# Whole V tile to the third buffer, all of wo to the first, in the tail of a decode-attention kernel

## The chip, the cores and the metric

The kernel runs on one core of one Trainium2 chip. The metric is device time in microseconds (us); the time shown for a version is the median of several executions. A profile is one further execution, recorded by the hardware profiler, and has a time of its own.

Engines are named as in the profile: PE is the matmul engine and PEld its weight load, DVE the vector engine, ACT the scalar engine, POOL the general one, SP the engine that issues nearly all transfers between HBM and on-chip memory. Each engine works through its own list of instructions in order; between engines, and between engines and transfers, order is kept by counters (semaphores) on which an instruction waits.

## The reference, cut to what matters

One decode step of a transformer block with attention and a feed-forward branch side by side: batch B = 4, one query each, D = 512, H = 32 heads of Dh = 128, a cache of Sk = 8192 keys and values per head, F = 1792, all bf16.

```python
xn = _layernorm(x)
q = (xn @ wq).reshape(B, 1, H, Dh).transpose(0, 2, 1, 3)
scores = einsum("bhqd,bhkd->bhqk", q, k_cache) * Dh ** -0.5
p = softmax(scores)
o = einsum("bhqk,bhkd->bhqd", p, v_cache)
attn = o.transpose(0, 2, 1, 3).reshape(B, 1, H * Dh) @ wo
ffn = (silu(xn @ w_gate) * (xn @ w_up)) @ w_down
out = x + attn + ffn
```

The K and V caches hold 537 MB together, and each of their elements is read once. Nearly all of the 550.77 MB that the kernel reads is theirs.

## The kernel before, in words

**Tiles.** The 128 pairs of batch and head are worked on in 32 head groups of four heads (`NT` = 32, `LAST` = 31). One group's K is one tile of 128 partitions by 32768 bf16 (64 KB a partition, 8.39 MB), and so is its V. Three buffers of that size, `slot[0]` to `slot[2]` (line 77), hold whatever is being loaded or used; K of group n and V of group n go to slot n mod 3, one after the other. Everything else is small.

**One step.** For group n, `begin` (line 353) turns K in place with DVE, piece by piece (`turn_k`, line 268), and PE computes the scores from each piece (`score`, line 275). Then `load_v` (line 97) issues the load of V into the slot that K has left. `finish` of the same group (line 364) takes the row maximum (`max_1`), multiplies the group before's probabilities with its V (`pv`, line 317: 64 matmuls, number k reading columns 512k to 512k+511 of the slot, the first 16 ahead of `max_2`, the other 48 behind it), issues the load of K of group n+2 into the slot that this V has left (`load_k`, line 94), and then turns its own probabilities (`pt_turn`) and finishes the group before's output (`fin`). So a step holds `finish(n)`, `begin(n+1)` and `load_v(n+1)`.

**Order and loop.** The order of the instructions is written out by hand (`manual_schedule`, line 70). The steps lie in a loop of 11 trips, n = 0, 3, ..., 30 (line 383). It has two arms: for n below 30, three steps (line 386); for n = 30, the tail (line 390), which holds the rest. All of SP's transfers go through one queue in program order, and each load of a slot waits until the slot's last readers are done.

**The waits.** The framework sets the waits. It follows which part of a buffer each instruction reads or writes, and makes a later access wait for an earlier one. A transfer's landing is seen by a completion counter; SP's transfers take eight counters in turn. At the loop's end both arms join, so that what the next trip meets is what either arm may have left. A wait that reaches across the loop's end is expressed as the value that the counter has when the trip before is over.

**The tail before.** `finish(30)` multiplies with V29 from slot 2. Then the first half of V31 (`va`, line 410) is loaded to the upper half of slot 2; once K31's first scores are done, its second half (`vb`, line 413) goes to the lower half of slot 1, and wo (`load_wo`, `load_wo_heads`, lines 396 and 400) in eight pieces to the lower half of slot 2, heads 0 to 31 at 512 columns each. Behind these loads in program order come the rest of group 30 (`max_1`, `pv` with V30 from slot 0, `max_2`, `fin`), `pv` with V31, and the output projection `wo_mm` (line 403), eight of whose heads stand between the two halves of the last `fin`. Two copies and two transfers write the result.

Of the kernel before, what the change touches and what calls it, by code (L numbers as in the profile page):

```python
# [15 lines left out]
def kernel(  # L16
# [13 lines left out]
    nc = tc.nc  # L30
    P = nc.NUM_PARTITIONS

    B, Sq, D = A_x.shape
    _, H, Sk, Dh = A_k_cache.shape
# [8 lines left out]
    T = HT * Sk // P  # L43
# [28 lines left out]
    def mm(out_ap, lhsT, rhs, start, **kw):  # L72
        nc.tensor.matmul(out_ap, lhsT=lhsT, rhs=rhs, start=start, stop=True,  # L73
                         skip_group_check=True, **kw)

    pad_t = pad.tile([P, 64], dt.bfloat16, name="pad_t")
    slot = [slots.tile([P, SLOT], dt.bfloat16, name=f"slot{i}") for i in range(NSLOT)]
    k_all = A_k_cache.rearrange("b (j h) (p t) d -> (b j) (h p) (t d)", h=HT, t=T)
    v_all = A_v_cache.rearrange("b (j h) (p t) d -> (b j) (h p) (t d)", h=HT, t=T)
# [17 lines left out]
    def load_v(n, s):  # L97
        nc.sync.dma_start(out=slot[s][:], in_=v_all[bass.ds(n, 1), :, :].rearrange("o p f -> (o p) f"))
# [5 lines left out]
                      in_=x_flat[B - 1:B, :].rearrange("b (k e) -> b k e", k=2))  # L104
# [43 lines left out]
    def yo_mm(lhsT, rhs, start=False):  # L148
        for i in range(2):
            mm(yo_ps[i][i * QB:i * QB + B, :], lhsT, rhs[:, i * DH:(i + 1) * DH], start=start)  # L150
# [39 lines left out]
    for half in range(NH):  # L190
        for par in range(2):
            src = q_ps[half][:].rearrange("p (x i r) -> p x i r", x=8, r=2)[:, :, :, par]
            src = src.unsqueeze(2).to_broadcast([P, 8, NQ, QB])
# [13 lines left out]
    for half in range(NH):  # L207
        for par in range(2):
            for a in range(HT):
                q0, q1 = a * QB, (a + 1) * QB  # L210
                nc.vector.tensor_copy(
                    out=qtn[q0:q1, :].rearrange("p (b h c j r) -> p h r j c b", b=B, h=NH, c=NQ, j=2)[:, half, par],
                    in_=qt_ps[q0:q1, half, par, 2 * a:2 * a + 2, :].rearrange("p j (c b) -> p j c b", b=B))
# [42 lines left out]
    NK = T // NV  # L256
    LAST = NT - 1
# [19 lines left out]
    def max_1():  # L277
        mx = small.tile([P, 1], dt.float32, name="mx")
        nc.vector.reduce_max(out=mx[:], in_=sps[:], axis=AX.X)  # L279
        return mx  # L280

    def max_2(mx):

        nc.tensor.matmul(mps[:, 0:P], lhsT=mx[:, 0:1].to_broadcast([P, P]), rhs=ident_f[:, :],  # L284
                         is_transpose=True, start=True, stop=True, skip_group_check=True)
        nm = small.tile([P, HT], dt.float32, name="nm")
        nc.vector.tensor_reduce(out=nm[:], in_=by_row(mps[:, 0:P]), axis=AX.X, op=ALU.max, negate=True)  # L287
        nc.vector.tensor_tensor(out=nm[:], in0=nm[:], in1=rowb_q[:], op=ALU.mult)
        nb = small.tile([P, 1], dt.float32, name="nb")
        nc.vector.reduce_sum(out=nb[:], in_=nm[:], axis=AX.X)  # L290
        rs = small.tile([P, 1], dt.float32, name="rs")
        nc.scalar.activation(out=p_[:], in_=sps[:], func=ACT.Exp, bias=nb[:, 0:1], scale=qscale,  # L292
                             accum_out=rs[:])
        return rs

    def pt_turn():
        for y in range(HT):
            nc.vector.transpose(out=ptz[y * QB:(y + 1) * QB, :, y, :, :].rearrange("p s u x -> p s (u x)"),  # L298
                                in_=p_[y * QB:(y + 1) * QB, :].rearrange("p (s w) -> p s w", s=4))
# [3 lines left out]
    def row_sums(rs):  # L303
        mm(mps[:, P:P + HT], rs[:, 0:1].to_broadcast([P, P]), rowb[:], start=True)

    def recip(c):
        nc.vector.reciprocal(out=rcp[c % NSLOT][:], in_=mps[:, P:P + HT])  # L307

    def p_off(k):
        g, s_ = divmod(k, TG // NV)  # L310
        return s_ * HT * NV * QB + 2 * g

    def pv(v, k0, k1):

        for k in range(k0, k1):
            q0, off = (k % NQ) * QB, p_off(k)
            mm(o_acc[q0:q0 + WR, :], pt[:, off:off + (WR - 1) * QB + 1:QB], v(k), start=(k < NQ))

    def in_slot(s):
        return lambda k: slot[s][:, k * 512:(k + 1) * 512]  # L320
# [17 lines left out]
    def fin(n, c, between=None):  # L338
        fin_1()
        if between:  # L340
            between()
        scaled(n, c, fin_2())

    def turned(j0, j1):

        xq = psX.tile([P, 4, B, j1 - j0], dt.float32, name="xps")
        src = otn_nat[:, HT:].rearrange("p (b j y) -> p b j y", b=B, y=HT)
        for y in range(HT):
            for c in range(4):
                mm(xq[y * QB:(y + 1) * QB, c, :, :], ident[:, c:P:4], src[:, :, j0:j1, y], start=(c == 0))  # L350
        nc.vector.tensor_copy(out=otn[:, j0 * 4:j1 * 4, :].rearrange("p (j c) b -> p c b j", c=4), in_=xq[:])

    def begin(n, c, parts=(4, 4, 2, 2, 2, 2), head=False):
        build_q(n)
        if head:
            mm(sps[0:1, 0:1], zq[:, 0, 0:1], zq[:, 0, 0:1], start=True)
        g0 = 0
        for w in parts:
            turn_k(c % NSLOT, g0, (w,))
            for g in range(g0, g0 + w):  # L360
                score(c % NSLOT, g)
            g0 += w

    def finish(n, c, load=True):
        sp = (c - 1) % NSLOT
        mx = max_1()
        pv(in_slot(sp), 0, 16)
        rs = max_2(mx)
        pv(in_slot(sp), 16, NK)
        if load:  # L370
            load_k(n + 2, sp)
        row_sums(rs)
        pt_turn()
        recip(c)
        fin(n - 1, c - 1)
# [7 lines left out]
    with tc.For_i(0, NT + 1, NSLOT, iteration_sync="reg_based", hint_engines=[]) as n:  # L383
        with tc.If(n < NT - 2) as turn:
            n = nc.s_assert_within(n, 0, NT - 2 - NSLOT, skip_runtime_bounds_check_because="the arm has n < NT - 2")
            for c in range(NSLOT):
                finish(n + c, c)
                begin(n + c + 1, c + 1)
                load_v(n + c + 1, (c + 1) % NSLOT)
        with turn.Else():  # L390
            finish(LAST - 1, LAST - 1, load=False)

            wo_t = slot[2]

            def load_wo(k0, k1):
                nc.sync.dma_start(out=wo_t[:, k0 * 4 * D:k1 * 4 * D].rearrange("p (k c e) -> p k (c e)", c=4, e=D),
                                  in_=A_wo[k0 * 4 * P:k1 * 4 * P, :].rearrange("(k p c) e -> p k (c e)", p=P, c=4))

            def load_wo_heads(h0, h1):
                nc.sync.dma_start(out=wo_t[:, h0 * D:h1 * D].rearrange("p (h e) -> p h e", e=D),  # L400
                                  in_=A_wo[h0 * P:h1 * P, :].rearrange("(h p) e -> p h e", p=P))

            def wo_mm(i):
                lhsT = otn[:, i, :] if i < H - HT else otn_nat[:, HT:].rearrange("p (b h) -> p b h", b=B)[:, :, i]
                yo_mm(lhsT, wo_t[:, i * D:(i + 1) * D])

            TH = T // 2
            va, vb = slot[2][:, H * D:H * D + TH * Dh], slot[1][:, 0:TH * Dh]
            src = v_all[LAST]
            nc.sync.dma_start(out=va, in_=src[:, 0:TH * Dh])  # L410
            turned(0, NB4 - 2)
            begin(LAST, LAST, (2,) * 8)
            nc.sync.dma_start(out=vb, in_=src[:, TH * Dh:T * Dh])
            for k0, k1 in ((0, 2), (2, 4), (4, 5), (5, 6), (6, 7)):
                load_wo(k0, k1)
            for h0, h1 in ((H - 4, H - 2), (H - 2, H - 1), (H - 1, H)):
                load_wo_heads(h0, h1)
            v30 = in_slot(0)
            mx = max_1()
            pv(v30, 0, 16)  # L420
            rs = max_2(mx)
            pv(v30, 16, NK)
            pt_turn()
            row_sums(rs)
            recip(LAST)
            fin(LAST - 1, LAST - 1)
            turned(NB4 - 2, NB4 - 1)
            v31 = lambda k: (va if k < NK // 2 else vb)[:, k % (NK // 2) * 512:(k % (NK // 2) + 1) * 512]
            pv(v31, 0, NK)
            fin(LAST, LAST, lambda: [wo_mm(i) for i in range(8)])  # L430
            for i in range(8, H):
                wo_mm(i)


            res = persist.tile([2 * QB, DH], dt.bfloat16, name="res")
            nc.vector.tensor_copy(out=res[0:B, :], in_=yo_ps[0][0:B, :])
            nc.scalar.copy(out=res[QB:QB + B, :], in_=yo_ps[1][QB:QB + B, :])
            nc.sync.dma_start(out=out_flat[:, 0:DH], in_=res[0:B, :])
            nc.scalar.dma_start(out=out_flat[:, DH:D], in_=res[QB:QB + B, :])
# [28 lines left out]
```

## Time and profile before

| | |
|---|---|
| median of 3 runs | 1444.53 us (1443.75 to 1447.37) |
| profiled execution: its time, its span | 1445.22 us, 1443.4 us |
| PE busy | 720.9 us (50%) |
| DVE busy | 788.3 us (55%) |
| ACT busy | 30.3 us (2%) |
| read from HBM | 550.77 MB, 382 GB/s over the span |
| mean granted PE clock | 0.746 |

The span runs from the first to the last instruction of the profiled execution; its own time is a little longer. In a row of the timeline the first number is the start in us from the span's start, the second how long the instruction or the merged group took; then come engine, line, operation, what is written and what is read, the count, and in brackets the idle time just before it with what ended it. Matmuls are issued by a helper at line 73 and are told apart by what they write: `sps` are scores, `oacc` the product with V, `yo_ps` the output. `SPq` rows are issues of transfers: L95 K, L98 V, L396 and L400 wo.

### The profile page before, as it was taken

Reading aid. Unit: us, or ns where it says so; the run is one execution under the profiler, and the core shown is the slowest. Engines: PE = TensorE matmul, PEld = TensorE weight load, DVE = VectorE, ACT = ScalarE, POOL = GpSimd, SP = SyncE. Lnnn points to the kernel's source line nnn. Section 1 sums busy time; section 2 is a strip of 40 time slices with the busy share of each in tenths; the row PEclk is TensorE's granted clock in tenths of the full one; section 3 lists DMA queues with packets and bytes.
Section 4 is the critical chain, followed back from the end, with each engine's and each line's share of the span. In section 5 each row is a group of like instructions: output and inputs, shape, how many; then the busy total and the mean of one; then the engine's idle time right before and its main releaser. Section 6 shows DMA issues by size and latency. Waiting matters only on the chain.

```text
span 1443.4 us, 11851 instructions
## 1 busy us (share of the span) xinstructions
PE 720.9 (50%) x4628; PEld 316.0 (22%) x4628; DVE 788.3 (55%) x756; ACT 30.3 (2%) x71; POOL 3.6 (0%) x11
## 2 busy tenths in 40 slices
PE   1765416734761654177157515542771564166436
PEld 0422102311320221033023202210330232022113
DVE  4567527725760774288166607833770676077334
ACT  1000000000000000000000000000000000000000
POOL 1000000000000000000000000000000000000000
PEclk9878757866885787588668858775886787577758
DMA  9999978997898799889968988998899699889965
GB/s 405 442 411 433 432 329 349 432 429 331 349 436 378 300 429 434 349 349 436 436 291 378 436 349 349 436 416 340 349 436 436 262 420 423 349 349 434 430 269 234
DMA packets 11509, 550.97 MB, mean 382 GB/s; under 512 B 1244, under 2 KB 1768, under 8 KB 2664
## 3 DMA queue, kind: packets, MB, share of 16 engines
q1 hardware_dynamic: 11488, 550.78, 89.3%
q8 instruction: 10, 0.16, 0.0%
q14 instruction: 3, 0.02, 0.0%
q10 hardware_dynamic: 8, 0.00, 0.0%
HBM read 550.77 MB, written 0.00 MB: 382 GB/s over the span
## 4 chain that ended last, share of the span: by engine, by line
PE 44%; DMA 31%; DVE 18%; issue 5%; PEld 1%; DVEq 0%; SPq 0%; ACT 0%; PEldq 0%
PE sps L73 32%; DMA slot<-in_A_v_cache_dram 26%; DVE slot L268 10%; PE oacc L73 9%; DMA slot<-in_A_k_cache_dram 5%; DVE ptz L298 3%; DVE oacc L330 1%; DVE o L331 1%; PE xps L73 1%; PE mps L73 1%; DVE zq L262 1%; PEld L73 1%; PE yo_ps L73 0%; DVE rcp L307 0%; PE mps L284 0%
## 5 line engine op out<-in xcount | busy, mean ns | idle before, releaser
L73 PE MATMUL sps<-slot,zq 128*128 128x512 bf16 x2048 | 510.3, 412 | 181.4 <-DVE slot L268 181.4
L268 DVE STREAM_TRANSPOSE slot<-slot 128x2048 uint32<-128x2048 uint32 (+1 forms) x196 | 561.6, 2929 | 3.5 <-DMA slot<-in_A_k_cache_dram 2.6
L298 DVE STREAM_TRANSPOSE ptz<-p__117 32x512 bf16<-32x512 bf16 x128 | 89.9, 703 | 460.8 <-PE mps L73 256.5
L73 PE MATMUL oacc<-slot,ptz 128*16 128x512 bf16 x2112 | 156.4, 444 | 356.6 <-DMA slot<-in_A_v_cache_dram 187.3
L73 PEld LDWEIGHTS <-zq 128*128 128x128 bf16 x2048 | 209.3, 103 | 469.4 <-issue 181.0
L73 PEld LDWEIGHTS <-ptz 128*16 128x16 bf16 x2112 | 61.1, 117 | 436.3 <-DMA slot<-in_A_v_cache_dram 192.3
L73 PE MATMUL xps<-rowy,o 128*128 128x4 f32 x66 | 18.9, 357 | 154.2 <-DVE o L331 154.2
L279 DVE TENSOR_REDUCE mx<-sps 128x1 f32<-128x512 f32 x32 | 22.1, 690 | 90.4 <-PE L73 66.1
L73 PEld LDWEIGHTS xps<-rowy,o 128*128 128x128 f32 x66 | 16.3, 307 | 157.0 <-DVE o L331 105.2
L292 ACT ACTIVATE p__117<-sps,nb 128x512 bf16<-128x512 f32 x32 | 22.0, 688 | 1338.1 <-DVE nb L290 1022.7
L330 DVE TENSOR_TENSOR oacc<-oacc,rowu 128x512 f32<-128x512 f32 x33 | 23.1, 700 | 5.6 <-PE yo_ps L73 4.6
L331 DVE TENSOR_REDUCE o<-oacc 128x128 f32<-128x512 f32 x33 | 22.8, 692 | 1.1
L262 DVE COPY zq<-qtn 32x4 bf16 (+1 forms) x128 | 21.7, 170 | 3.0
L287 DVE TENSOR_REDUCE nm<-mps 128x4 f32<-128x64 f32 x32 | 7.2, 225 | 24.9 <-PE L73 12.7
L326 DVE TENSOR_TENSOR otn_nat<-xps,rcp 128x4 f32 (+1 forms) x33 | 5.4, 163 | 22.9 <-PE xps L73 21.0
L73 PEld LDWEIGHTS mps<-rowb,rs 128*128 128x128 f32 x64 | 10.5, 205 | 15.5 <-issue 15.5
L73 PE MATMUL mps<-rowb,rs 128*128 128x4 f32 x64 | 13.3, 278 | 0.0
L284 PE MATMUL mps<-ident_f,mx 128*128 128x128 f32 x32 | 10.6, 332 | 5.2 <-DVE mx L279 5.2
L73 PEld LDWEIGHTS <-slot 128*128 128x128 bf16 (+1 forms) x172 | 9.5, 143 | 5.6 <-DVE slot L195 2.7
L284 PEld LDWEIGHTS mps<-ident_f,mx 128*128 128x128 f32 x32 | 4.3, 136 | 19.0 <-DVE mx L279 18.1
L382 DVE MEMSET slot<- 128x5632 uint32 x1 | 4.8, 4752 | 4.5 <-issue 4.5
L73 PE MATMUL yo_ps<-slot,ident 4*4 4x256 bf16 x2 | 0.4, 366 | 13.1 <-DMA slot<-in_A_x_dram 13.1
(59 smaller groups left out, 71.7 us busy)
## 6 DMA issues: line engine op xcount, KB each, us to landing
slot<-in_A_v_cache_dram SPq DMA_DIRECT2D x2, 4096.0 KB, 12.0
slot<-in_A_wq_dram SPq DMA_DIRECT2D x1, 4096.0 KB, 12.2
slot<-in_A_wo_dram SPq DMA_DIRECT2D x2, 1024.0 KB
slot<-in_B_w_gate_dram SPq DMA_DIRECT2D x1, 1792.0 KB, 16.6
slot<-in_B_w_up_dram SPq DMA_DIRECT2D x1, 1792.0 KB, 19.6
slot<-in_B_w_down_dram SPq DMA_DIRECT2D x1, 1792.0 KB, 23.7
slot<-in_A_wo_dram SPq DMA_DIRECT2D x3, 512.0 KB, 18.8
slot<-in_A_k_cache_dram SPq DMA_DIRECT2D x32, 36.5
```

What stands on the lines that cost most here:

```text
L73: nc.tensor.matmul(out_ap, lhsT=lhsT, rhs=rhs, start=start, stop=True, skip_group_check=True, **kw)
L262: nc.vector.tensor_copy(out=zq[q0:q1, :, XO + a * QB], in_=qtn[q0:q1, bass.ds(n * 4, 4)])
L268: nc.vector.transpose(out=ap, in_=ap)
L279: nc.vector.reduce_max(out=mx[:], in_=sps[:], axis=AX.X)
L284: nc.tensor.matmul(mps[:, 0:P], lhsT=mx[:, 0:1].to_broadcast([P, P]), rhs=ident_f[:, :], is_transpose=True, start=True, stop=True, skip_gr ...
L287: nc.vector.tensor_reduce(out=nm[:], in_=by_row(mps[:, 0:P]), axis=AX.X, op=ALU.max, negate=True)
L292: nc.scalar.activation(out=p_[:], in_=sps[:], func=ACT.Exp, bias=nb[:, 0:1], scale=qscale, accum_out=rs[:])
L298: nc.vector.transpose(out=ptz[y * QB:(y + 1) * QB, :, y, :, :].rearrange("p s u x -> p s (u x)"), in_=p_[y * QB:(y + 1) * QB, :].rearrange ...
L326: nc.vector.tensor_tensor(out=otn_nat[:, bass.ds((n + 1) * HT, HT)], in0=xps[:], in1=rcp[c % NSLOT][:], op=ALU.mult)
L330: nc.vector.tensor_tensor(out=o_, in0=o_, in1=rowu[:].unsqueeze(2).to_broadcast([P, NV, Dh]), op=ALU.mult)
L331: nc.vector.reduce_sum(out=o1[:], in_=o_.rearrange("p u d -> p d u"), axis=AX.X)
L382: nc.vector.memset(slot[2][:, 2 * EC * F + FC * D:], 0.0)
```

## The change

In the tail, V31 is loaded by `load_v(LAST, 2)`, one transfer of the whole tile to slot 2, where before two halves went to slots 2 and 1. wo goes to slot 0 instead of slot 2, in the same eight pieces to the same columns, and its loads are moved in program order from behind `begin(LAST)` to behind the product with V30, which is what slot 0 holds until then. The product with V31 reads slot 2 alone. Nothing else is edited; the loop's other arm is the same text.

```diff
-            wo_t = slot[2]
+            wo_t = slot[0]
...
-            TH = T // 2
-            va, vb = slot[2][:, H * D:H * D + TH * Dh], slot[1][:, 0:TH * Dh]
-            src = v_all[LAST]
-            nc.sync.dma_start(out=va, in_=src[:, 0:TH * Dh])
+            load_v(LAST, 2)
             turned(0, NB4 - 2)
             begin(LAST, LAST, (2,) * 8)
-            nc.sync.dma_start(out=vb, in_=src[:, TH * Dh:T * Dh])
-            for k0, k1 in ((0, 2), (2, 4), (4, 5), (5, 6), (6, 7)):
-                load_wo(k0, k1)
-            for h0, h1 in ((H - 4, H - 2), (H - 2, H - 1), (H - 1, H)):
-                load_wo_heads(h0, h1)
             v30 = in_slot(0)
             mx = max_1()
             pv(v30, 0, 16)
             rs = max_2(mx)
             pv(v30, 16, NK)
+            for k0, k1 in ((0, 2), (2, 4), (4, 5), (5, 6), (6, 7)):
+                load_wo(k0, k1)
+            for h0, h1 in ((H - 4, H - 2), (H - 2, H - 1), (H - 1, H)):
+                load_wo_heads(h0, h1)
             pt_turn()
...
-            v31 = lambda k: (va if k < NK // 2 else vb)[:, k % (NK // 2) * 512:(k % (NK // 2) + 1) * 512]
-            pv(v31, 0, NK)
+            pv(in_slot(2), 0, NK)
```

## The prediction, made before the changed kernel had run

> **What bounds the kernel now.** I read the page first, then the list of waits, then the timeline trip by trip, and the tail last.
>
> ```profile
> DMA  9999978997898799889968988998899699889965
> GB/s 405 442 411 433 432 329 349 432 429 331 349 436 378 300 429 434 349 349 436 436 291 378 436 349 349 436 416 340 349 436 436 262 420 423 349 349 434 430 269 234
> HBM read 550.77 MB, written 0.00 MB: 382 GB/s over the span
> L73 PE MATMUL oacc<-slot,ptz 128*16 128x512 bf16 x2112 | 156.4, 444 | 356.6 <-DMA slot<-in_A_v_cache_dram 187.3
> ```
>
> The slices are 36 us long. The first five run at 405 to 442 GB/s, and from the sixth on every second or third falls to about 340. So the transfers are the widest resource, and they pause at regular intervals. The other half of the story is that the PV matmuls (line 317, shown under the helper's L73) idle 356.6 us waiting for transfers. The list of waits says how often:
>
> ```profile
> PE oacc L73 <- DMA slot<-in_A_v_cache_dram: 187.3, 10, 18.8
> PE oacc L73 <- DMA slot<-in_A_k_cache_dram: 163.1, 10, 17.7
> ```
>
> Ten times each, in 33 PV products: once per return of the loop (trips begin at n = 0, 3, ..., 30, so ten returns). One trip, n = 27, in the timeline:
>
> ```profile
> 1216.44 1.06 PE L73 MATMUL oacc<-slot,ptz 128*16 128x512 bf16 x16
> 1216.54 0.33 SPq L98 DMA_DIRECT2D slot<-in_A_v_cache_dram  x1
> 1235.14 0.62 PE L73 MATMUL oacc<-slot,ptz 128*16 128x512 bf16 x4 [17.38 <-DMA slot<-in_A_k_cache_dram]
> 1254.56 1.90 PE L73 MATMUL oacc<-slot,ptz 128*16 128x512 bf16 x16 [18.80 <-DMA slot<-in_A_v_cache_dram]
> 1259.72 0.33 SPq L95 DMA_DIRECT2D slot<-in_A_k_cache_dram  x1
> 1286.91 1.06 PE L73 MATMUL oacc<-slot,ptz 128*16 128x512 bf16 x16
> 1287.12 0.33 SPq L98 DMA_DIRECT2D slot<-in_A_v_cache_dram  x1
> 1288.16 2.79 PE L73 MATMUL oacc<-slot,ptz 128*16 128x512 bf16 x48
> 1291.51 0.33 SPq L95 DMA_DIRECT2D slot<-in_A_k_cache_dram  x1
> 1318.24 1.06 PE L73 MATMUL oacc<-slot,ptz 128*16 128x512 bf16 x16
> 1349.26 1.06 PE L73 MATMUL oacc<-slot,ptz 128*16 128x512 bf16 x16
> ```
>
> Steps two and three of a trip do their PV as 16 and 48 matmuls and take 31.3 us (1286.91 to 1318.24) and 31.0. Step one stops after 16 matmuls until 1235.14, does 4, and stops until 1254.56. That product reads V26 from slot 2, whose first 16 matmuls ran at once, so V26 was there. The transfer that lands at 1254.56 is V27, issued at 1216.54, for slot 0. The product waits for data that it does not read. Meanwhile K29 cannot be issued (slot 2 is not free) before 1259.72, and nothing is queued behind V27:
>
> ```profile
> 1254.60:1259.80 5.20, 4.80 (x46) 1.76 (x46) 0.38 (x1) 0.00 (x0) 0.00 (x0) 0.62 0.00 0
> ```
>
> (columns: PE, PEld, DVE, ACT, POOL busy, clock, DMA share, GB/s: zero). A second hole follows when K29 lands, at about 1281, before V28 is issued at 1287.12.
>
> **Where the false wait comes from.** Matmul k reads columns 512k to 512k+511, so the stops are at columns 8192 and 10240. Those are exactly where the tail's wo pieces (4,5) and (5,6) begin in slot 2. The framework joins both arms of the branch at the loop's end, so the first reader of a slot in the next trip must also wait for what the tail arm writes there. Its waits are on completion counters: SP's transfers take eight in turn, and both arms start with counter 0. In the loop arm K(slot 2), V(slot 1), K(slot 0), V(slot 2), K(slot 1), V(slot 0) take 0 to 5. In the tail arm va and vb take 0 and 1, wo's pieces 2, 3, 4, 5, 6, 7, 0, 1. So piece (4,5) shares counter 4 with K for slot 1, piece (5,6) shares 5 with V for slot 0: the two youngest transfers of the trip before. The instruction list of the kernel before carries these waits, on counters 4 and 5 at PV matmuls 16 and 20, and the trace's 16/4/44 split agrees.
>
> **The change, part by part.** (1) The tail arm now writes slot 2 with one transfer, V31, the arm's first: counter 0. In the loop arm counter 0 is the K load of step one, landed two steps earlier. So step one's PV keeps only its true wait, for V in slot 2. (2) wo goes to slot 0, on counters 1 to 7 and 0. The loop first reads slot 0 in step two's PV, which needs V there (counter 5) anyway, and step one's transposes have already waited for K in slot 1 (counter 4). The old values of the other counters were reached a trip before. These added waits cost nothing; their cover is that step two comes 31 us or more after the return. If they were on transfers of the current trip instead, they would cost what rival 1 says. (3) vb goes, and with it a tail write to slot 1.
>
> What a loop without the stop runs at: the transfers' rate. Step two's work (31.3) is shorter than two transfers. With three slots, V of head group n can be issued about 20.5 us after K of n lands (transposes at 1297.68 below, scores done at 1318.24), while the queue is busy for 38.8 us after that landing (V of n-1, then K of n+1); the next K is issued 4.5 us later. So the queue always holds work, with some 18 us to spare.
>
> ```profile
> 1297.68 17.54 DVE L268 STREAM_TRANSPOSE slot<-slot 128x4096 uint32<-128x4096 uint32 x6
> 145.19 17.54 DVE L268 STREAM_TRANSPOSE slot<-slot 128x4096 uint32<-128x4096 uint32 x6 [0.54 <-DMA slot<-in_A_k_cache_dram]
> 184.14 0.62 PE L73 MATMUL oacc<-slot,ptz 128*16 128x512 bf16 x4 [10.60 <-DMA slot<-in_A_k_cache_dram]
> 203.42 4.44 PE L73 MATMUL oacc<-slot,ptz 128*16 128x512 bf16 x44 [18.66 <-DMA slot<-in_A_v_cache_dram]
> 1386.33 4.89 PE L73 MATMUL oacc<-slot,ptz 128*16 128x512 bf16 x44 [18.68 <-DMA slot<-in_A_v_cache_dram]
> 85.00:200.00 115.00, 60.74 (x351) 25.85 (x351) 63.38 (x54) 2.34 (x6) 0.00 (x0) 0.75 0.99 427
> 1290.00:1385.00 95.00, 40.56 (x242) 17.51 (x234) 47.95 (x44) 1.56 (x4) 0.00 (x0) 0.73 0.99 430
> ```
>
> The first trip has no stop, and shows the state: K3 lands at 145.19 and DVE takes it at once, so there the transfers bind. Price of 8.39 MB: K3 (145.19) to V3 (203.42), three transfers without a hole, 58.23, or 19.41 each; V3 alone 19.28; 95 us at 430 GB/s give 19.51. I take 19.40, bounds 19.28 and 19.51.
>
> From K3 to V30 there are 57 transfers (V2 to V30, K4 to K31). Before: 145.19 to 1386.33, 1241.1 us. Without holes: 57 x 19.40 = 1105.8, so V30 lands at 1251.0 (1244 to 1257). That saves 135.3, or 15.0 per trip: nine trips from 203.42 to 1386.33 take 131.4 each, against 6 x 19.40 = 116.4.
>
> **The tail.** Before:
>
> ```profile
> 1391.84 0.35 SPq L410 DMA_DIRECT2D slot<-in_A_v_cache_dram  x1
> 1410.77 0.34 SPq L413 DMA_DIRECT2D slot<-in_A_v_cache_dram  x1
> 1411.27 2.61 SPq L396 DMA_DIRECT2D slot<-in_A_wo_dram  x5
> 1413.93 9.16 SPq L400 DMA_DIRECT2D slot<-in_A_wo_dram  x3
> slot<-in_A_v_cache_dram SPq DMA_DIRECT2D x2, 4096.0 KB, 12.0
> 1432.00:1434.00 2.00, 2.00 (x36) 1.12 (x32) 0.00 (x0) 0.00 (x0) 0.00 (x0) 0.84 0.27 92
> 1418.97 1.06 PE L73 MATMUL oacc<-slot,ptz 128*16 128x512 bf16 x16
> 1420.22 2.79 PE L73 MATMUL oacc<-slot,ptz 128*16 128x512 bf16 x48
> 1429.18 5.33 PE L73 MATMUL oacc<-slot,ptz 128*16 128x512 bf16 x64
> 1438.87 0.60 PE L73 MATMUL yo_ps<-slot,otn_nat 128*4 128x256 bf16 x8
> 1440.21 0.62 ACTq L439 DMA_DIRECT2D out_dram<-res  x1
> ```
>
> Here compute sets the end: 57.1 us from V30's landing to 1443.4, half of it the work on K31, which lay finished in slot 1 during the stop. After the change that work runs under V30's transfer: K31 lands at 1231.6, its scores are done about 20.5 later, V31 was issued long before (after PV of V29) and lands one transfer after V30, at 1270.4. PV of V30 starts at about 1252 and is over 4.0 us later (as 1418.97 to 1423.0), so the eight wo issues reach the queue near 1257, at most 12 us of issuing (1411.27 to 1423.1), all but the last behind V31. That last piece reuses counter 0 and is issued when V31 lands; the pieces ahead of it cover that. wo takes 9.7 us (vb landed at 1410.77 + 12.0 = 1422.8, traffic ends at about 1432.5): 1280.1. On PE, PV of V31 to the last wo matmul takes 10.3 us (1429.18 to 1439.47): 1280.7. The two ends nearly meet; I take the later. Behind it lie 3.9 us of casts and output (1439.47 to 1443.4): **1284.6**, that is 33.6 us after V30 instead of 57.1, 23.5 less. On SP only the output is queued behind wo.
>
> Sum: 135.3 + 23.5 = 158.8. The profiled run took 1445.22, 1.8 over its span of 1443.4; it is 0.7 over the median of 1444.53. So 1444.5 - 158.8 = **1286** (1279 to 1293 by the price of a transfer alone).
>
> Two rules of the Trainium skill speak against this sum. "DMA: Bandwidth & Descriptors", section "Where 436 GB/s comes from", says that loads from HBM are bound by the HBM side at about 358 GB/s per core; 550.77 MB would then take an estimated 1538 us, more than the kernel takes already, and the 115 us at 427 GB/s contradict it for one core alone. The same page, "Anatomy of one DMA", adds a fixed 2.0 us to each transfer's bytes; if queued transfers paid it one by one, 57 of 21.2 us (an estimate) would end about 105 us later, near 1391. The trace's 19.28 from one queued landing to the next shows that the fixed part is hidden once something is queued.
>
> **Rivals.** 1: *The stop moves with wo.* wo's counters sit on slot 0 now; if step two's PV had to wait for the current trip's youngest transfers (K of n+2, V of n+1), it would stop as step one does today, 131 us per trip as now. The tail alone gains nothing visible, since from 1386.33 on nothing there waits for a transfer. About 1444. Against it: the old waits are for values of the trip before, as the landings at 1235.14 and 1254.56 show. 2: *Two stops per trip*, the slower side. If slot 0's readers stop as in rival 1 and V31 leaves one in slot 2, each trip has the hole twice: 10 x 15.0 more, 1594. It decides only if V31's counter also belonged to a young transfer; the count above gives it counter 0, the oldest. 3: *The transfers tire.* The longest stretch without a hole in the trace is 115 us; if an unbroken 1100 us only held the span's mean of 382 GB/s, a transfer costs 21.96, V30 lands at 1396.9 and the end is about 1432. For it only: no longer stretch was seen. The trace's rate at its end (430) equals that at its start, so little.
>
> **Chances.** Forecast 0.87, rival 1 0.06, rival 2 0.03, rival 3 or a smaller share of it 0.04. A measurement tells 0.3%, 4.3 us, from no change. Faster 0.91, same 0.06, slower 0.03. Range 1277 to 1306: below, 57 x 0.12 = 7 us cheaper transfers and a little; above, 6 us dearer ones, up to 3 us for wo's last pieces, and 1 us lost at each of ten returns.
>
> **What would show it.** Right: no PV matmul split into 16, 4 and 44; about 19.4 us between landings throughout; DVE's transposes waiting for K in nearly every step; slices near 430 GB/s up to the end; V31's PV waiting for its transfer. Wrong: oacc still waiting ten times for two transfers, now at another slot's product; a zero-GB/s hole in each trip; or slices that all sag below 400.

## The result, and the profile after

The changed kernel takes 1282.51 us (median of 4 runs, 1281.04 to 1284.07) against 1445.1 us for the kernel before in the same comparison: a ratio of 0.8874, 95% interval 0.8858 to 0.889. The forecast was 1286 us, range 1277 to 1306. Its profiled execution has a span of 1280.9 us and took 1282.67.

The page of the changed kernel, the lines that answer to those shown of before:

```profile
DMA  9999999999999999999999999999999999999998
GB/s 401 454 424 400 429 427 444 432 434 426 444 432 434 426 448 428 434 430 444 428 434 434 442 428 432 440 436 430 430 442 434 434 426 444 432 434 426 445 430 339
HBM read 550.77 MB, written 0.00 MB: 430 GB/s over the span
L268 DVE STREAM_TRANSPOSE slot<-slot 128x2048 uint32<-128x2048 uint32 (+1 forms) x196 | 561.6, 2929 | 194.3 <-DMA slot<-in_A_k_cache_dram 194.2
L73 PE MATMUL oacc<-slot,ptz 128*16 128x512 bf16 x2112 | 133.9, 398 | 14.7 <-DMA slot<-in_A_v_cache_dram 9.0
```

The slices that fell to about 340 GB/s within the run are gone; the last one, at 339, holds the end. The PV matmuls' idle time fell from 356.6 to 14.7 us. What waits for transfers now is DVE, ahead of turning K: 194.3 us. Where one wait went, another has come, but of another kind, as the list of waits shows:

```profile
DVE slot L268 <- DMA slot<-in_A_k_cache_dram: 194.2, 29, 8.0
PE oacc L73 <- DMA slot<-in_A_v_cache_dram: 9.0, 1, 9.0
```

It is spread over 29 of the 32 head groups with at most 8.0 us each, and DVE waits for exactly the K that it is about to turn. That is what a kernel bound by its transfers looks like. The PV wait is one, for V31 in the tail. Three steps in a row, so that the first step of a trip is among them:

```profile
1055.89 1.06 PE L73 MATMUL oacc<-slot,ptz 128*16 128x512 bf16 x16
1057.14 2.79 PE L73 MATMUL oacc<-slot,ptz 128*16 128x512 bf16 x48
1073.42 17.54 DVE L268 STREAM_TRANSPOSE slot<-slot 128x4096 uint32<-128x4096 uint32 x6 [6.78 <-DMA slot<-in_A_k_cache_dram]
1093.98 1.06 PE L73 MATMUL oacc<-slot,ptz 128*16 128x512 bf16 x16
1095.22 2.79 PE L73 MATMUL oacc<-slot,ptz 128*16 128x512 bf16 x48
1132.12 1.06 PE L73 MATMUL oacc<-slot,ptz 128*16 128x512 bf16 x16
1133.37 2.79 PE L73 MATMUL oacc<-slot,ptz 128*16 128x512 bf16 x48
```

Every product goes 16 and 48, none 16, 4 and 44. The steps start about 38 us apart. The landing of K3, the landing of V31, the end, and two windows (columns as before: PE, PEld, DVE, ACT, POOL busy, clock, DMA share, GB/s):

```profile
146.13 17.54 DVE L268 STREAM_TRANSPOSE slot<-slot 128x4096 uint32<-128x4096 uint32 x6 [0.63 <-DMA slot<-in_A_k_cache_dram]
1267.02 5.02 PE L73 MATMUL oacc<-slot,ptz 128*16 128x512 bf16 x64 [9.01 <-DMA slot<-in_A_v_cache_dram]
1276.43 0.82 PE L73 MATMUL yo_ps<-slot,otn_nat 128*4 128x256 bf16 x8
145.00:1267.00 1122.00, 615.18 (x3889) 270.11 (x3890) 695.79 (x641) 22.59 (x58) 0.00 (x0) 0.76 1.00 434
1267.00:1276.60 9.60, 8.56 (x126) 5.30 (x126) 1.55 (x3) 0.00 (x0) 0.00 (x0) 0.85 0.91 363
```

For 1122 us the transfers run at 434 GB/s without a hole. 58 transfers (V2 to V31, K4 to K31) take 1267.02 - 146.13 = 1120.9 us, 19.33 each.

### The profile page after: what moved, and what is told of

Its sections match the earlier page's. It is cut to its first block, busy times and chain, and to the rows that moved or that the text cites. A ratio compares the mean times of both kernels' runs of the same rounds, so it can differ in the third digit from the quotient of the medians.

```text
span 1280.9 us, 11827 instructions
## 1 busy us (share of the span) xinstructions
PE 706.6 (55%) x4628; PEld 314.9 (25%) x4628; DVE 789.8 (62%) x756; ACT 30.3 (2%) x71; POOL 3.6 (0%) x11
## 4 chain that ended last, share of the span: by engine, by line
PE 44%; DVE 17%; another core or an unknown queue 14%; DMA 6%; issue 5%; PEld 0%; DVEq 0%; ACT 0%; PEldq 0%; SPq 0%
PE sps L73 33%; DVE slot L268 9%; PE oacc L73 8%; DMA slot<-in_A_k_cache_dram 3%; DVE ptz L298 3%; DMA slot<-in_A_v_cache_dram 3%; DVE oacc L330 1%; DVE o L331 1%; PE xps L73 1%; DVE zq L262 1%; PE mps L73 1%; PE mps L284 1%; PEld L73 0%; DVE rcp L307 0%
## 5 line engine op out<-in xcount | busy, mean ns | idle before, releaser
L73 PE MATMUL sps<-slot,zq 128*128 128x512 bf16 x2048 | 520.3, 418 | 372.4 <-DVE slot L268 372.4
L268 DVE STREAM_TRANSPOSE slot<-slot 128x2048 uint32<-128x2048 uint32 (+1 forms) x196 | 561.6, 2929 | 194.3 <-DMA slot<-in_A_k_cache_dram 194.2
L73 PE MATMUL oacc<-slot,ptz 128*16 128x512 bf16 x2112 | 133.9, 398 | 14.7 <-DMA slot<-in_A_v_cache_dram 9.0
```

The source lines that it names most:

```text
L268: nc.vector.transpose(out=ap, in_=ap)
```

## The experiments

The theory on trial, as it went into the first runs: step one of a trip stopped because the tail arm writes slot 2 with transfers on counters 4 and 5, which the youngest K and V of the trip before also use. Its rivals: that it matters where wo lies, or how the tail orders its loads; and, for the price, that each stop costs its own length. The table has three groups of four rows; the runs of each group shared one chip and the runs of the kernel before (1445.5, 1445.65 and 1445.55 us).

| run | against | us, median | ratio to before, 95% interval |
|---|---|---|---|
| e1: wo in two pieces | before | 1286.24 | 0.8902 (0.8887 to 0.8917) |
| e2: V31 in six | changed | 1282.1 | 0.8871 (0.8856 to 0.8886) |
| e3: V31 in five | changed | 1281.87 | 0.8872 (0.8857 to 0.8887) |
| e4: va in three | before | 1282.99 | 0.8875 (0.886 to 0.889) |
| e5: wo in slot 1 | changed | 1294.47 | 0.8951 (0.8938 to 0.8965) |
| e6: wo moved alone | before | 1281.73 | 0.8869 (0.8856 to 0.8883) |
| e7: zeros earlier | changed | 1281.3 | 0.8864 (0.8852 to 0.8876) |
| changed kernel again | | 1282.29 | 0.8869 (0.8857 to 0.8881) |
| e8: V31 in six, wo in four | changed | 1413.55 | 0.9774 (0.9758 to 0.979) |
| e9: V31 in five, wo in four | changed | 1283.6 | 0.8879 (0.8865 to 0.8894) |
| e10: output in four | before | 1282.98 | 0.8873 (0.8859 to 0.8888) |
| e11: output in three | before | 1445.47 | 0.9998 (0.9988 to 1.0007) |

**e1: the counters alone, wo still in slot 2.**

```diff
-            for k0, k1 in ((0, 2), (2, 4), (4, 5), (5, 6), (6, 7)):
-                load_wo(k0, k1)
-            for h0, h1 in ((H - 4, H - 2), (H - 2, H - 1), (H - 1, H)):
-                load_wo_heads(h0, h1)
+            load_wo(0, 7)
+            load_wo_heads(H - 4, H)
```

> The kernel before, with one edit: wo is loaded in two transfers instead of eight, still to slot 2, still ahead of the rest of group 30; V31 still comes in two halves. The tail then uses counters 0 and 1 for the halves and 2 and 3 for wo, so counters 4 and 5 stay off slot 2. Counter theory: no stop in step one, the loop runs at the transfers' rate, 1280 to 1290 us, and no product split into 16, 4 and 44. Rival, the place of wo: if the next trip's reader of slot 2 is held up because the tail writes wo there, whatever the counter, 1440 to 1450. Rival, the order of the tail's loads: if V31 in one piece and wo behind V30 are what helps, 1440 to 1450 too.

Measured 1286.24 us, without a stop. Wo lies where it lay, in the order in which it was; the rivals fall. On the same chip e4 below, which keeps wo in eight pieces, took 1282.99. The 3.3 us that e1 takes longer have a row: the first projection matmul must wait for all 28 heads' worth of wo in one piece.

```profile
1274.45 1.87 PE L73 MATMUL yo_ps<-slot,otn 128*4 128x256 bf16 x16 [5.08 <-DMA slot<-in_A_wo_dram]
```

**e6: one part of the change alone.** V31 stays in halves, wo goes to slot 0 behind the product with V30.

```diff
-            wo_t = slot[2]
+            wo_t = slot[0]
...
-            for k0, k1 in ((0, 2), (2, 4), (4, 5), (5, 6), (6, 7)):
-                load_wo(k0, k1)
-            for h0, h1 in ((H - 4, H - 2), (H - 2, H - 1), (H - 1, H)):
-                load_wo_heads(h0, h1)
             v30 = in_slot(0)
...
             pv(v30, 16, NK)
+            for k0, k1 in ((0, 2), (2, 4), (4, 5), (5, 6), (6, 7)):
+                load_wo(k0, k1)
+            for h0, h1 in ((H - 4, H - 2), (H - 2, H - 1), (H - 1, H)):
+                load_wo_heads(h0, h1)
```

> One part of the change alone: wo to slot 0 and behind the product with V30, V31 still in two halves in slots 2 and 1. Counters 4 and 5 then stay off slot 2. Counter theory: as the changed kernel, 1280 to 1290; the single transfer of V31 is worth nothing by itself. Rival, the single transfer of V31 carries the gain: 1430 to 1450.

Measured 1281.73 us, not to be told from the changed kernel's 1282.29 beside it. The single transfer of V31 is worth nothing that can be measured.

**e2 and e4: stops put back or moved by shifting the counters.** In e2 the changed kernel loads V31 in pieces:

```diff
-            load_v(LAST, 2)
+            for i in range(6):
+                c0, c1 = i * T // 6 * Dh, (i + 1) * T // 6 * Dh
+                nc.sync.dma_start(out=slot[2][:, c0:c1], in_=v_all[LAST][:, c0:c1])
```

> The changed kernel, with one edit: V31 is loaded to slot 2 in six transfers instead of one. They take counters 0 to 5, so the fifth and sixth, at columns 21760 and 27264, share counters 4 and 5 with the youngest K and V of the trip before. Counter theory: step one's product stops at matmul 42 until K lands and at matmul 53 until V lands. Only 11 matmuls are left behind the second landing instead of 44, so K is issued about 3.2 us earlier than in the kernel before: a trip of about 128 us instead of 131.4, 1405 to 1420 in all. Rivals of place or order: wo is in slot 0 and behind V30, so 1280 to 1290.

In e4 the kernel before loads `va` in three:

```diff
-            nc.sync.dma_start(out=va, in_=src[:, 0:TH * Dh])
+            for c0, c1 in ((0, TH // 4 * Dh), (TH // 4 * Dh, TH // 2 * Dh), (TH // 2 * Dh, TH * Dh)):
+                nc.sync.dma_start(out=va[:, c0:c1], in_=src[:, c0:c1])
```

> The kernel before, with one edit: the first half of V31 comes in three transfers instead of one. That moves each piece of wo two counters on: the pieces at columns 0 and 4096 now take counters 4 and 5. Counter theory: the stops move from matmuls 16 and 20 to matmuls 0 and 8; behind the second landing 56 matmuls and the maximum's step are left instead of 44, about 1.2 us more in each trip, 1448 to 1465. Rivals that do not go by counters: the split stays at 16 and 20 and the time at 1440 to 1450.

Measured 1282.1 and 1282.99 us: no stop in either, against my theory. The waits of e4, a kernel with wo in slot 2 and counters 4 and 5 on its first columns:

```profile
DVE slot L268 <- DMA slot<-in_A_k_cache_dram: 195.4, 29, 8.1
PE oacc L73 <- DMA slot<-in_A_v_cache_dram: 5.3, 1, 5.3
```

So a shared counter is not enough. The instruction lists of the kernels, which no view of the profile shows, have what differs. In e2 and e4 the tail arm uses counters 4 and 5 twice, the loop arm once. Both arms must leave a counter at the same value, so the framework adds 16, the value of one transfer, to the loop arm by an instruction of SP, ahead of the loop's own transfer. A wait for the tail's first transfer on the counter is then met by this filler and no longer stands for K or V. In the kernel before, counters 4 and 5 are used once in each arm: no filler, and the wait for the tail's piece of wo is in truth a wait for K or V. My mended theory: the stop needs a piece that is the tail's last on its counter, on a counter whose value the loop arm reaches only with a young transfer.

**e3** was to price one of the two stops and had the same flaw:

```diff
-            load_v(LAST, 2)
+            for i in range(5):
+                c0, c1 = i * T // 5 * Dh, (i + 1) * T // 5 * Dh
+                nc.sync.dma_start(out=slot[2][:, c0:c1], in_=v_all[LAST][:, c0:c1])
```

> The changed kernel with V31 in five transfers, on counters 0 to 4. Step one's product must stop once, at matmul 51, until the youngest K of the trip before has landed, and not for V. Counter theory together with the reading that only a held-back issue costs: the stop is there ten times, 10 us or more each, but the next K is issued while V is still under way, so the transfers never run dry: 1281 to 1290. Rival, each stop costs its length: 10 times 10 to 17 us more, 1385 to 1450.

Measured 1281.87 us, but with no stop at all: the time fits, the reading behind it was not tested.

**e10 and e11: the mended theory at its barest.** All loads are those of the kernel before. Only the output's 4 KB are written in more transfers, which gives counters 4 and 5 (e10) or counter 4 alone (e11) a second use in the tail: by the instruction lists the output's writes, ACT's among them, take the next counters in turn, 2 and 3 in the kernel before, 2 to 5 in e10 and 2 to 4 in e11.

```diff
-            nc.sync.dma_start(out=out_flat[:, 0:DH], in_=res[0:B, :])
-            nc.scalar.dma_start(out=out_flat[:, DH:D], in_=res[QB:QB + B, :])
+            nc.sync.dma_start(out=out_flat[:, 0:DH // 2], in_=res[0:B, 0:DH // 2])
+            nc.sync.dma_start(out=out_flat[:, DH // 2:DH], in_=res[0:B, DH // 2:DH])
+            nc.scalar.dma_start(out=out_flat[:, DH:DH + DH // 2], in_=res[QB:QB + B, 0:DH // 2])
+            nc.scalar.dma_start(out=out_flat[:, DH + DH // 2:D], in_=res[QB:QB + B, DH // 2:DH])
```

(e11: the first of the two lines alone is split.)

> The kernel before with all its loads as they are, wo in slot 2 in eight pieces and V31 in halves; only the output is written in four transfers of 1 KB instead of two of 2 KB. The two more take counters 4 and 5, which so get a second transfer in the tail arm and a filler ahead of the loop's own transfer. Mended counter theory: the stop vanishes, 1280 to 1290. Any theory of where wo lies, in what order it is loaded, or into how many pieces V31 is cut: 1440 to 1450.

> The kernel before with the output in three transfers. Counter 4 gets a filler, counter 5 does not. Mended counter theory: the stop at matmul 16 for K is gone and the one at matmul 20 for V stays; since V lands behind K, the time stays as before, 1438 to 1450, with the product split into 20 and 44 instead of 16, 4 and 44. If the stop for K cost something of its own: 10 us or more less.

Measured 1282.98 us for e10: two more writes of 1 KB at the very end of the program, and the whole gain of the change is there. e10's waits:

```profile
DVE slot L268 <- DMA slot<-in_A_k_cache_dram: 197.1, 29, 8.1
PE oacc L73 <- DMA slot<-in_A_v_cache_dram: 5.3, 1, 5.3
```

e11 took 1445.47 us, ratio 0.9998 (0.9988 to 1.0007). Its first step of a trip, in the timeline, and its line in the list of waits:

```profile
1219.17 1.06 PE L73 MATMUL oacc<-slot,ptz 128*16 128x512 bf16 x16
1220.42 0.42 PE L73 MATMUL oacc<-slot,ptz 128*16 128x512 bf16 x4
1256.03 4.89 PE L73 MATMUL oacc<-slot,ptz 128*16 128x512 bf16 x44 [35.19 <-DMA slot<-in_A_v_cache_dram]
PE oacc L73 <- DMA slot<-in_A_v_cache_dram: 352.5, 10, 37.2
```

The stop at matmul 16 is gone: the 4 run right behind the 16 (the maximum's step lies between them), and the whole wait, 352.5 us, now ends with V. Of the two stops the one for V alone made the time.

**e8 and e9: the stops put back into the changed kernel.** As e2 and e3, with wo in four transfers (`(0, 2), (2, 4), (4, 7)` and the last four heads), so that the tail uses counters 4 and 5, or 4, once.

> As the run with V31 in six transfers, but wo in four transfers instead of eight, so that counters 4 and 5 have one transfer each in the tail arm, as they have in the loop arm, and get no filler. Mended counter theory (a wait across the loop's end stops only where the tail's transfer is the last on its counter and the loop arm's own transfer stands for the same value): the stop comes back, in slot 2 and with wo in slot 0, at matmuls 42 and 53 of step one's product. 11 matmuls instead of 44 are left behind the second landing, some 3.2 us a trip less than in the kernel before: 1400 to 1430. If sharing a counter has nothing to do with it: 1280 to 1292, as with eight pieces of wo.

> As the run with V31 in five transfers, but wo in four, so that counter 4 has one transfer in each arm and counter 5 is not in slot 2. Mended counter theory: step one's product stops at matmul 51 until the youngest K has landed, ten times, and not for V. With the reading that only a held-back issue costs, the transfers never run dry and nothing is lost: 1281 to 1290. If each stop costs its length, 10 times 10 to 17 us more: 1385 to 1450.

Measured 1413.55 us for e8. One trip's first step:

```profile
1195.06 1.71 PE L73 MATMUL oacc<-slot,ptz 128*16 128x512 bf16 x26
1211.37 1.48 PE L73 MATMUL oacc<-slot,ptz 128*16 128x512 bf16 x11 [14.60 <-DMA slot<-in_A_k_cache_dram]
1230.67 1.47 PE L73 MATMUL oacc<-slot,ptz 128*16 128x512 bf16 x11 [17.83 <-DMA slot<-in_A_v_cache_dram]
1232.69 0.33 SPq L95 DMA_DIRECT2D slot<-in_A_k_cache_dram  x1
```

The stops are at matmuls 42 (16 + 26) and 53, where the fifth and sixth piece of V31 begin. K is issued 2.0 us after V lands instead of 5.2, and the kernel is 32.0 us faster than before: the 3.2 us a trip that were forecast. The stops lasted 325 us in all (146.3 for K and 178.7 for V in the list of waits), and the kernel is 131 us slower than e10, which has none. So what a stop costs is not its length but the issue that it holds back.

e9 took 1283.6 us. It stops too:

```profile
1110.93 1.90 PE L73 MATMUL oacc<-slot,ptz 128*16 128x512 bf16 x13 [15.45 <-DMA slot<-in_A_k_cache_dram]
1113.27 0.33 SPq L95 DMA_DIRECT2D slot<-in_A_k_cache_dram  x1
PE oacc L73 <- DMA slot<-in_A_k_cache_dram: 136.7, 10, 15.5
```

Ten stops, 136.7 us in all, and no time lost that can be measured: e10, on the same chip and without a stop, took 1282.98. K is issued at 1113.27, while V is still on its way for another 17 us (an estimate: K landed at 1110.93, and V lands 19.33 behind it). The list of waits alone would have named this, the kernel's largest wait for a transfer, as the thing to remove.

**e5: a false wait on another engine.** The changed kernel, wo in slot 1 and loaded right behind the scores of K31.

```diff
-            wo_t = slot[0]
+            wo_t = slot[1]
...
             begin(LAST, LAST, (2,) * 8)
+            for k0, k1 in ((0, 2), (2, 4), (4, 5), (5, 6), (6, 7)):
+                load_wo(k0, k1)
+            for h0, h1 in ((H - 4, H - 2), (H - 2, H - 1), (H - 1, H)):
+                load_wo_heads(h0, h1)
...
             pv(v30, 16, NK)
-            for k0, k1 in ((0, 2), (2, 4), (4, 5), (5, 6), (6, 7)):
-                load_wo(k0, k1)
-            for h0, h1 in ((H - 4, H - 2), (H - 2, H - 1), (H - 1, H)):
-                load_wo_heads(h0, h1)
```

> The changed kernel, with wo in slot 1 instead of slot 0, its loads issued right behind the scores of K31. Slot 1's first reader in the next trip is DVE, which turns K there in step one; wo's fifth piece shares counter 5 with the youngest V. So the second of DVE's pieces must wait until that V has landed, about 15 us, once a trip. Counter theory with the reading that only a held-back issue costs: the scores are done about 35.4 us after K's landing, V is issued some 3 us before the transfers run dry, and the delay of 15 us is made up in the next two steps: 1281 to 1292, with DVE seen waiting ten times for a V transfer. Rival, each false wait costs its length: about 150 us more, 1420 to 1440.

Measured 1294.47 us. The false wait is there, on DVE, and in the tail once more:

```profile
204.92 13.22 DVE L268 STREAM_TRANSPOSE slot<-slot 128x4096 uint32<-128x4096 uint32 x5 [14.62 <-issue]
1139.67 13.22 DVE L268 STREAM_TRANSPOSE slot<-slot 128x4096 uint32<-128x4096 uint32 x5 [15.05 <-DMA slot<-in_A_v_cache_dram]
1156.67 0.33 SPq L98 DMA_DIRECT2D slot<-in_A_v_cache_dram  x1
1159.00:1165.00 6.00, 1.82 (x30) 0.90 (x22) 3.76 (x7) 0.33 (x2) 0.00 (x0) 0.99 0.81 350
1237.71 6.70 DVE L268 STREAM_TRANSPOSE slot<-slot 128x2048 uint32<-128x2048 uint32 x3 [6.98 <-DMA slot<-in_A_k_cache_dram]
1257.00 11.09 DVE L268 STREAM_TRANSPOSE slot<-slot 128x2048 uint32<-128x2048 uint32 x5 [12.59 <-issue]
1280.56 5.49 PE L73 MATMUL oacc<-slot,ptz 128*16 128x512 bf16 x64
DVE slot L268 <- DMA slot<-in_A_v_cache_dram: 120.0, 8, 15.2
DVE slot L268 <- issue: 27.2, 2, 14.6
```

The list names V for eight of the stops; the two that it puts down to "issue", at 204.92 and at 1257.00, stand before the same piece, so all ten are there, nine in the loop and one in the tail. The rival's 1420 to 1440 is far off. But my reading that the delay is made up was not quite right either, and the range was missed by 2.5 us. In the changed kernel K31 is taken at 1228.09:

```profile
1228.09 17.66 DVE L268 STREAM_TRANSPOSE slot<-slot 128x2048 uint32<-128x2048 uint32 x8 [5.63 <-DMA slot<-in_A_k_cache_dram]
```

In e5 it is 1237.71, ahead of the tail's stop. From K3's landing (146.86 in e5) to there e5 needs 1090.9 us and the changed kernel 1082.0, so the nine stops in the loop cost 8.9 us, about 1 us each. The trip shown has the place: V28 is issued at 1156.67, only 2.3 us before K29 lands (an estimate: 1139.67 + 19.33 = 1159.0), and in the six us from there the transfers' share is 0.81, which is 1.1 us without traffic; at the same place in the seven trips before it is 0.81 to 0.92. The tail's stop of 12.59 us costs about 4 us more: from K31's landing to the end e5 takes 57.1 us (1237.71 to 1294.8), the changed kernel 52.8 (1228.09 to 1280.9).

**e7: something better?** The changed kernel's only slice near 400 GB/s within the run is the fourth. DVE's zeros were moved ahead of the feed-forward branch.

```diff
+    W3 = 2 * EC * F + FC * D
+    nc.vector.memset(slot[2][:, W3 + 8 * FC * B:], 0.0)
     do_ffn()
-    nc.vector.memset(slot[2][:, 2 * EC * F + FC * D:], 0.0)
+    nc.vector.memset(slot[2][:, W3:W3 + 8 * FC * B], 0.0)
```

> The changed kernel, with DVE's 4.75 us of zeros in slot 2 ahead of the feed-forward branch instead of behind it (a small rest stays behind). DVE is idle there. The first maximum and all behind it come up to 4.7 us earlier, V1 is issued before K2 has landed, and the hole between 96 and 128 us (400 GB/s there) closes: 1 to 2.5 us less than the changed kernel, 1279 to 1282. If that hole has another cause, no change.

> The changed kernel once more, on the same chip as the three runs beside it: 1280 to 1285.

Measured 1281.3 against 1282.29 us on the same chip; the intervals of the ratios overlap, so by the time no gain is shown. The window from 96 to 128 us shows the hole closing, first in the changed kernel run again, then in e7:

```profile
96.00:128.00 32.00, 21.67 (x139) 9.62 (x138) 24.40 (x24) 0.78 (x2) 0.00 (x0) 0.84 0.97 410
```

```profile
96.00:128.00 32.00, 21.68 (x151) 9.60 (x149) 24.60 (x23) 0.78 (x2) 0.00 (x0) 0.84 0.99 429
```

19 GB/s over 32 us are 0.6 MB, or 1.4 us at 434 GB/s: about the size of the difference of the medians, too small for the measurement.

## Why the prediction was right, and where it was not

**The stop and its end.** Right: in the changed kernel no product is split, and the loop runs at the transfers' rate. That the gain is in the loop's other arm, whose text is the same, e10 shows most plainly.

**The rule behind it.** The step "piece (4,5) shares counter 4 with K for slot 1, piece (5,6) shares 5 with V for slot 0", given as the reason for the stop, was too short. e2 and e4 share the counters and do not stop; e8 to e11 show that the value counts as well. The instruction lists of all the kernels above agree with the mended theory: every kernel that stops has, on the columns where it stops, a piece on counter 4 or 5 and no filler on that counter. Of those that do not stop, e2, e3, e4 and e10 have fillers on both counters, and in the changed kernel, e1 and e6 slot 2 has no piece on either. V31's counter 0 in the changed kernel has a filler too, so its wait is met even ahead of the K load that the prediction named. The description of the waits ahead of the prediction is too coarse in the same place: the value waited for is that of the tail's own transfer, which need not be the last value of the trip. It made no difference for the forecast, since both kernels use counters 4 and 5 once in each arm, and the change takes them off slot 2. That the rule as I had it was enough for this change was luck: of e2 and e4, judged by the same rule, I forecast 1405 to 1420 and 1448 to 1465 us, wrong by 120 to 180.

**The counters of slot 0.** Right: in the changed kernel two of wo's pieces sit on counters 4 and 5 in slot 0, and nobody is seen to wait for them; e5 shows counter 5 in slot 1 being waited for. Rivals 1 and 2 are out.

**The price of a transfer.** Taken 19.40, measured 19.33: over 58 transfers that is 4.3 us less (1120.9 against 1125.2). K3 landed 0.9 later than before (146.13), and the stretch from V31's landing to the end took 13.9 instead of 14.2. Together these are the 3.7 us by which the span came out under the forecast (1280.9 against 1284.6). Rival 3, that transfers tire, is out: 434 GB/s over 1122 us.

On that point the Trainium skill, "DMA: Bandwidth & Descriptors", section "Where 436 GB/s comes from", is of two minds. Its ceiling of 435.2 GB/s for the ports agrees with the 434 measured here; its statement that loads from HBM are bound at about 358 GB/s per core does not hold for this run on one core. The measurement decides. The prediction's other figure from that page, the fixed 2.0 us of "Anatomy of one DMA" in the Trainium skill, is a fit for transfers that GpSimd issues, and these are issued by SP. Here 58 queued transfers of 8.39 MB took 19.33 us each, which is 434 GB/s with no such part seen.

If 434 GB/s is as fast as these transfers go, only the start, the last 14 us and about one hole in the first 130 us are left to gain.

**The tail.** The forecast of 23.5 us was right in sum. V30 landed at about 1247.7 (1267.02 - 19.33), 33.2 us before the end; forecast were 33.6, before 57.1. e6 and e10, which keep V31 in halves, are as fast, and e10 keeps the tail's order too. So the edit of the tail earns nothing by itself; the tail got shorter because the work on K31 no longer waits out a stop. SP issued wo from 1248.53 on and its last piece at 1267.05, when V31 had landed, as forecast; the wait hid.

**What stays open.** The fillers stand in the instruction lists, not in the traces; the traces show which waits are there. Why the framework fixes its waits in this way was not looked into. How early a load must be issued for no time to be lost is known at two points only: 17 us ahead nothing is lost that can be measured (e9), 2.3 us ahead about 1 us a trip is (e5).

## What to carry to other kernels

When an engine waits for a transfer that it does not read, look at which columns it stops and which other code writes those columns, even code that runs once at the end: a loop's branch joined at the back edge lets the last trip's buffers and the number of its transfers slow every trip. A false wait costs only what it keeps from being issued: here ten stops of 13.7 us cost nothing that can be measured (e9), nine of 15 us that let the next load go only just ahead of time cost 1 us each (e5), and in the kernel before, where the next load went out after the queue had run dry, the stops cost 163 us with what they added to the tail. Before a tail is rearranged for such a reason, try the cheapest edit that only shifts the counters; here two 1 KB writes did it.

## What the runs showed that was not expected

Splitting the output's two writes of 2 KB into four of 1 KB made the kernel 163 us faster (e10, 1445.55 to 1282.98 us), and into three nothing (e11): the completion counters are part of a kernel's timing as much as its loads. And the queue held 434 GB/s for 1122 us while DVE and PE were busy 62% and 55% of the span. DVE turns one K in 17.54 us in both kernels.
